# Seven half-size products for eight in the last block of a fused retention and bilinear feed-forward kernel

## The chip, the cores and the metric

The kernel runs on one core of a Trainium2 chip. The metric is the device time of one execution in microseconds. A core has five engines with queues of their own that run side by side and wait for each other through semaphores: TensorE (PE in the profile, its weight loads PEld), VectorE (DVE), ScalarE (ACT), GpSimd (POOL) and SyncE (SP), which here only starts transfers. TensorE writes into PSUM, a small memory of eight banks; GpSimd works only on SBUF, the large one.

## The reference

Retention without softmax over 8 batches, 8 heads, 576 positions and 64 values per head, then a bilinear feed-forward layer over all 4608 tokens:

```
scores = scale * q @ k.T                        # per batch and head
ret    = (scores * decay[h] ** (i - j), i >= j) @ v
x      = ret as (4608, 512)                     # heads side by side
a      = x @ w_a                                # (512, 1536)
b      = x @ w_b                                # (512, 1536)
out    = (a * b) @ w_out                        # (1536, 512)
```

Inputs and output are f32; the kernel multiplies in bf16 and sums in f32.

## The kernel before

Tokens are taken in blocks (512, 256, 256, then seven of 512). `ffn_block` does the feed-forward layer of one block. Between its steps it hands out the retention work of later blocks, which a list `todo` places by a count of matmuls: one unit is a matmul of 512 columns, and an entry is called at the first edge (end of an F step, or of a block) at or after its place. All engines' queues follow the order in which the program emits instructions.

For a block of 512 tokens, with xT the tokens' x, transposed (128 rows x 4 parts x 512):

- First product. For each of 12 columns F of w_a and w_b (128 wide): 4 matmuls into pa (L1141), a copy to bf16 by ScalarE (ha, L1152), 4 matmuls into pb (L1159), and VectorE multiplies the two into hT[:, F] (L1164). That is 96 matmuls of 512 columns a block.
- Row sums. From the seventh block of 256 tokens on, the second product takes seven products for eight (Strassen's scheme in Winograd's form, on quarters of h and w_out). It needs sums of h rows: `row_sums` (L944, recorded on L952) makes five VectorE instructions: three into hsum, two that change hT in place. In the block, they are made for pairs of F 0 to 3 after F = 7 and for pairs 4 and 5 after the last F. `work` hands them out from the list `jobs` within a budget.
- Second product. `rows_mixed` (L982) runs 84 matmuls of 256 columns (`product`, L1022) for two groups g of 256 tokens. The order is: products 3 and 4 on plain h rows, product 1 on the first row sum, then `cross(g)`: products 5 and 2 on the changed h rows; ScalarE keeps what they gave ("crossed", L1034), GpSimd adds the kept "straight" part into the output tile osb (L1045), VectorE subtracts (`lessen`, L1055) and adds the rest (`add_last`, L1062), and SP stores the tile (L972). "straight", "crossed" and "less" are tiles with two buffers each.

In the stretch that matters here, the block before last, retention ends: `outputs_alone` writes the last x rows through VectorE (L808) after F = 9 of that block, in steps taken from the list `later` at F = 10. GpSimd's own retention work, the casts of `ahead` (L562 to L589), is over well before; after it GpSimd has two osb adds per block left. The last block has no retention work beside it.

The stage buffers (tags qf, kf, vf, three each) held the loaded q, k and v of earlier token groups; the last of these loads stands ahead of the last two blocks.

Of the kernel before, what the change touches and what calls it, by code (L numbers as in the profile page):

```python
# [18 lines left out]
def kernel(  # L19
# [10 lines left out]
    nc = tc.nc  # L30
# [4 lines left out]
    NTOK = B * S  # L35
    NC = DM // 128
# [8 lines left out]
    NP = NTOK // 256  # L45
# [34 lines left out]
    stage = pool("stage", 3)  # L80
    nat = pool("nat", 3)
# [5 lines left out]
    ha_pool = pool("ha", 6)  # L87
    o_pool = pool("osb", 4)
    late, early = {}, ExitStack()
# [13 lines left out]
    ps_ffn = pool("ps_ffn", 4, PS)  # L103
    opening, ps_sc, ps_o = ExitStack(), {}, {}
# [17 lines left out]
    wa_sb = big.tile([128, NC, DFF], BF16)  # L122
    wb_sb = big.tile([128, NC, DFF], BF16)
# [18 lines left out]
    shared = {}  # L142
# [117 lines left out]
    def pair_tables(step):  # L260
# [6 lines left out]
        else:  # L267
            for h in (2 * step - 2, 2 * step - 1):
# [33 lines left out]
    def pop():  # L302
        if later:
            later.pop(0)()

    jobs, copies_due = [], []

    def work(budget, up_to=2):
        jobs.sort(key=lambda job: job[0])
        while jobs and jobs[0][0] <= up_to and jobs[0][1] <= budget:  # L310
            _, cost, job = jobs.pop(0)
            job()
            budget -= cost
# [615 lines left out]
    WIDE = DM // 2  # L929
# [11 lines left out]
        out = wo_sums[:, step // 3, p0:p0 + 2]  # L941
        nc.vector.tensor_tensor(out, one, other, op=op)

    def row_sums(hT, sums, p0, p1):  # L944

        even, odd = (hT[:, 2 * p0:2 * p1].rearrange(
            "p (f e) (g k s) -> p e k f g s", e=2, g=2, k=2)[:, e]
            for e in (0, 1))
        a11, a21, a12, a22 = even[:, 0], even[:, 1], odd[:, 0], odd[:, 1]
        to = [sums[:, i, p0:p1] for i in range(3)]  # L950
        return [(1, (p1 - p0) / 8 + 0.2,
                 lambda e=e: nc.vector.tensor_tensor(*e[:3], op=e[3]))  # L952
                for e in ((to[0], a11, a22, ALU.add),
                          (to[2], a12, a22, ALU.subtract),
                          (to[1], a21, a11, ALU.subtract),
                          (a12, a11, a12, ALU.add),
                          (a21, a21, a22, ALU.add))]

    def store_mixed(G, osb, cols=slice(0, 2 * DM), on=nc.sync):

        n = place(G)
        for kp, r0, m, b, s0 in rows_of(n):
            if n in LEFT:
                p0 = kp * 64 + r0 // 2
                m //= 2
            elif kp == 1:
                continue
            else:
                p0, m = 0, 128
            rows = out[b * S + s0:b * S + s0 + 2 * m].rearrange(  # L970
                "(p two) c -> p (two c)", two=2)
            on.dma_start(rows[:, cols],  # L972
                              osb[p0:p0 + m].rearrange("p k c -> p (k c)")
                              [:, cols])
# [3 lines left out]
    def store_formed():  # L978
        while formed:
            store_mixed(*formed.pop(0))  # L980

    def rows_mixed(tok0, hT, sums):  # L982
# [129 lines left out]
            formed.append((pair[g], osbs[g]))  # L1112
        yield 0, True

    def ffn_block(tb, tok0, n, runs):

        xT = x_of(tok0, n)
        hT = h_pool.tile([128, NF, 512], BF16, tag="h", name="hT")
        if tok0 >= 256 * MIXED:
            pools_mixed()  # L1120
            sums = late["hsum"].tile([128, 3, NF // 2, 2, 128], BF16, tag="hsum",
                                  name="hsum")
        f0 = 0
        for count in runs:
            has = {}
            if tb == 0 and f0 == 0:
                for c in range(2, NC):
                    for F in range(count):
                        begin_with(F, c, 1)
            for F in range(f0, f0 + count):  # L1130
                fs = slice(F * 128, (F + 1) * 128)
                pa = (begun[F] if tb == 0 and F in begun else
                      ps_ffn.tile([128, 512], FP32, tag="ab", name="pa"))
                for c in range(NC):
                    if tb == 0 and (F, 0, 0) in begun:
                        if (F, c, 1) not in begun:
                            begin_with(F, c, 1)
                        if c < NC - 1:
                            yield n / 512, False
                        continue  # L1140
                    nc.tensor.matmul(pa[:, 0:n], wa_sb[:, c, fs],  # L1141
                                     xT[:, c],
                                     start=(c == 0), stop=(c == NC - 1))
                    if c < NC - 1:
                        yield n / 512, False
                if n == 512 and tb:
                    pop()
                pass_on(1)
                if F == 2:
                    store_formed()  # L1150
                ha = ha_pool.tile([128, 512], BF16, tag="ha", name="ha")
                nc.scalar.copy(ha[:, 0:n], pa[:, 0:n])  # L1152
                has[F] = ha
                yield n / 512, False
            for F in range(f0, f0 + count):
                fs = slice(F * 128, (F + 1) * 128)
                pb = ps_ffn.tile([128, 512], FP32, tag="ab", name="pb")
                for c in range(NC):
                    nc.tensor.matmul(pb[:, 0:n], wb_sb[:, c, fs],  # L1159
                                     xT[:, c],  # L1160
                                     start=(c == 0), stop=(c == NC - 1))
                    if c < NC - 1:
                        yield n / 512, False
                nc.vector.tensor_tensor(hT[:, F, 0:n], has[F][:, 0:n],  # L1164
                                        pb[:, 0:n], op=ALU.mult)
                pop()
                if tok0 >= 256 * MIXED:
                    if F == 7:
                        jobs.extend(row_sums(hT, sums, 0, 4))
                    elif F == NF - 1:  # L1170
                        jobs.extend(row_sums(hT, sums, 4, 6))
                        work(math.inf, 1)
                work(1.0)
                yield n / 512, True
            f0 += count
        if tb == 0:
            yield from rows_together(tok0, hT, (0, 1))
# [122 lines left out]
    starts, at = {}, 0.0  # L1300
# [42 lines left out]
    def third_turn():  # L1343
        for i in (4, 5):
            transpose_step(i, (Q, "act"), (K, "dve"))

    todo = [(100, early_casts, ()),
            (112.1, cast_step, (5, Q, "act")),
            (124, third_turn, ()), (128, third_states, ()),
            (136, third_outputs, ())]  # L1350
# [34 lines left out]
        casts[n], turns[n] = placed[n] - 96, placed[n] - 58  # L1385
    for fn, places in ((ahead, casts), (turn, turns)):
        todo += [(at, fn, (n,)) for n, at in places.items()]
    todo.sort(key=lambda e: e[0])

    at = 0.0  # L1390
    tok = 0
    for tb, n in enumerate(blocks):
        runs = WCOLS if tb == 0 else [1] * NF
        for cost, edge in ffn_block(tb, tok, n, runs):
            at += cost
            while todo and edge and at >= todo[0][0]:
                _, fn, args = todo.pop(0)
# [33 lines left out]
```

## Time and profile before

Times are microseconds.

| what | value |
|---|---|
| median of 3 runs | 322.25 (321.19 to 322.4) |
| the profiled execution, whole | 320.63 |
| its span, first to last instruction | 318.4 |
| granted TensorE clock in it | 1.000 |
| PE, DVE, ACT, POOL busy | 308.0, 198.9, 145.7, 155.6 |

The page gives busy time by engine, then the same in 40 slices of the span as digits (9 is 90% or more), then the chain of work that ended last, then groups of instructions by line. A group's row reads: line, engine, operation, output <- inputs, output shape and type <- input shape and type, count, busy time, mean length of one. In the trace's timeline the first number is the start in the span, the second the length of the row's instructions together. A start-to-start distance can be a little shorter than a length, as instructions of one engine overlap at their ends.

### The profile page before, as it was taken

To read this page: it belongs to the slowest core of one execution; us is meant where nothing else is said; L and a number is where in the kernel's file an instruction comes from. 1 tells how busy PE (TensorE), PEld (TensorE's weight loads), DVE (VectorE), ACT (ScalarE), POOL (GpSimd) and SP (SyncE) were. 2 spreads that over 40 slices of the span, in tenths; PEclk is the share of its full clock that TensorE was granted. 3 is DMA by queue.
4 is the path that set the end of the run, shared out by engine and by line. 5 is a ranking of instruction groups with operands and counts; after the bars stand their busy time and mean duration, and the time that the engine had idled before them with its cause. 6 is when DMAs were issued, how large, how long until landed. Compare 5 with 4: busy or idle time off the path is not lost.

```text
span 318.4 us, 9134 instructions
## 1 busy us (share of the span) xinstructions
PE 308.0 (97%) x3763; PEld 183.4 (58%) x3799; DVE 198.9 (62%) x376; ACT 145.7 (46%) x324; POOL 155.6 (49%) x169
## 2 busy tenths in 40 slices
PE   7899999999999999999999999999999999999995
PEld 3554457768544554448654864477446744674474
DVE  5745346867757563479658854776567656834563
ACT  7745346536435463454454534544434443423330
POOL 3990078664986577564796089506960300030003
PEclk9999999999999999999999999999999999999999
DMA  8999999999999999999999998974430110012004
GB/s 215 255 203 207 255 231 184 193 207 182 207 178 214 229 218 179 240 193 223 241 280 201 179 229 181 198 164 129 108 68 2 76 61 0 2 74 60 0 1 132
DMA packets 144793, 50.92 MB, mean 160 GB/s; under 512 B 126576, under 2 KB 141680, under 8 KB 144752
## 3 DMA queue, kind: packets, MB, share of 16 engines
q1 hardware_dynamic: 138272, 45.10, 70.9%
q0 software_dynamic: 5808, 4.72, 9.4%
q8 instruction: 29, 0.48, 0.6%
q10 hardware_dynamic: 672, 0.52, 0.5%
q14 instruction: 12, 0.10, 0.1%
HBM read 37.75 MB, written 9.44 MB: 148 GB/s over the span
## 4 chain that ended last, share of the span: by engine, by line
PE 90%; DVE 3%; DMA 2%; issue 2%; POOL 1%; SPq 1%; ACT 0%; DVEq 0%; POOLq 0%
PE pb L1159 29%; PE pa L1141 28%; PE m L1022 16%; PE po L1185 8%; DMA vf<-in_v_dram 2%; PE po L913 2%; PE sc L703 1%; PE o L731 1%; PE o L744 1%; SPq L175 1%; PE kv L632 1%; DVE hT L952 1%; POOL vb L365 1%; DVE sums L659 1%; PE pa L902 1%
## 5 line engine op out<-in xcount | busy, mean ns | idle before, releaser
L1164 DVE TENSOR_TENSOR hT<-ha,pb 128x512 bf16<-128x512 bf16 (+1 forms) x120 | 75.8, 632 | 80.4 <-PE pb L1159 68.5
L1159 PE MATMUL pb<-xT,wb_sb 128*128 128x512 bf16 (+1 forms) x478 | 111.5, 358 | 0.4
L1152 ACT CAST ha<-pa 128x512 bf16<-128x512 f32 (+1 forms) x120 | 64.9, 542 | 96.8 <-PE pa L1141 92.0
L1141 PE MATMUL pa<-xT,wa_sb 128*128 128x512 bf16 (+1 forms) x448 | 106.4, 356 | 1.9 <-issue 1.2
L1159 PEld LDWEIGHTS <-wb_sb 128*128 128x128 bf16 x480 | 46.8, 98 | 47.5 <-issue 1.9
L1141 PEld LDWEIGHTS <-wa_sb 128*128 128x128 bf16 x472 | 45.0, 98 | 43.0 <-DVE sums L659 0.2
L1045 POOL TENSOR_TENSOR osb<-crossed,straight 128x512 f32<-128x512 f32 x12 | 15.2, 1271 | 102.8 <-ACT crossed L1034 96.3
L589 POOL TENSOR_TENSOR vb<-vf,vs 128x1024 bf16<-128x1024 f32 (+1 forms) x17 | 29.6, 1743 | 4.5 <-PE pb L1159 1.7
L1022 PEld LDWEIGHTS <-hT 128*128 128x128 bf16 x288 | 28.1, 98 | 4.7 <-issue 0.3
L562 POOL TENSOR_TENSOR qkb<-qf,qs 64x1024 bf16<-64x1024 f32 x12 | 22.9, 1911 | 14.2 <-DMA qf<-in_q_dram 9.1
L1185 PE MATMUL po<-wo_sb,hT 128*128 128x512 bf16 x113 | 26.7, 379 | 0.8 <-issue 0.6
L1022 PE MATMUL m<-wo_sums,hsum 128*128 128x256 bf16 x216 | 25.7, 273 | 0.0
L567 POOL TENSOR_TENSOR qkb<-qf,qs 64x512 bf16<-64x512 f32 x24 | 24.8, 1052 | 0.7
L1022 PEld LDWEIGHTS <-hsum 128*128 128x128 bf16 x216 | 21.1, 98 | 2.4
L952 DVE TENSOR_TENSOR hsum<-hT 128x1024 bf16<-128x1024 bf16 (+1 forms) x36 | 20.3, 591 | 0.2
L578 POOL CAST qkb<-kf 64x1024 bf16<-64x1024 f32 (+1 forms) x17 | 15.9, 935 | 8.0 <-DMA kf<-in_k_dram 7.1
L712 DVE TENSOR_TENSOR sT<-sc,mask 128x512 bf16<-128x512 f32 x30 | 19.8, 680 | 0.0
L659 DVE TENSOR_TENSOR sums<-kv,sums 128x256 f32<-128x256 f32 x44 | 18.6, 422 | 1.4
L582 POOL CAST qkb<-kf 64x512 bf16<-64x512 f32 (+1 forms) x34 | 18.8, 581 | 0.9
L1185 PEld LDWEIGHTS <-hT 128*128 128x128 bf16 x120 | 11.2, 98 | 12.6
L1022 PE MATMUL m<-wo_sb,hT 128*128 128x256 bf16 x144 | 17.0, 273 | 0.1
L1022 PE MATMUL m<-wo_sums,hT 128*128 128x256 bf16 x144 | 16.9, 273 | 0.0
(111 smaller groups left out, 283.0 us busy)
## 6 DMA issues: line engine op xcount, KB each, us to landing
qf<-in_q_dram SPq DMA_DIRECT2D x32, 256.0 KB, 5.1
vf<-in_v_dram SPq DMA_DIRECT2D x32, 256.0 KB, 5.2
kf<-in_k_dram SPq DMA_DIRECT2D x31, 256.0 KB, 4.9
out_dram<-osb SPq DMA_DIRECT2D x9, 512.0 KB, 4.1
out_dram<-osb SPq DMA_DIRECT2D x22, 128.0 KB, 2.8
wo_sb<-in_moe_w_out_dram POOLq DMA_DIRECT2D x3, 512.0 KB, 16.0
out_dram<-osb SPq DMA_DIRECT2D x6, 256.0 KB, 4.2
qf<-in_q_dram SPq DMA_DIRECT2D x8, 128.0 KB, 4.2
```

Of the source, the lines that this page charges most:

```text
L562: nc.gpsimd.tensor_tensor(per_head(qkb[0:64, Q]), per_head(t[0:64]), by[0:64].unsqueeze(2).to_broadcast([64, 2 * H, D]), op=ALU.mult)
L567: nc.gpsimd.tensor_tensor(per_head(qkb[64:128, Q])[:, 1 - r::2], per_head(t[64:128])[:, r::2], by[64:128, r::2].unsqueeze(2).to_broadcast( ...
L589: nc.gpsimd.tensor_tensor(vb[:, e].rearrange("p (h d) -> p h d", d=D), t[:, e].rearrange("p (h d) -> p h d", d=D), decay[:, at], op=ALU.mult)
L659: nc.vector.tensor_tensor(sums[:, i], own, prev, op=ALU.add)
L712: nc.vector.tensor_tensor(sT[:, on].rearrange("p c k s -> p (c k) s"), sc[on].rearrange("p c k s -> p (c k) s"), mask3.unsqueeze(1).to_bro ...
L952: lambda e=e: nc.vector.tensor_tensor(*e[:3], op=e[3]))
L1022: nc.tensor.matmul(to, rows, cols, start=(begins and p == 0), stop=True, skip_group_check=True)
L1141: nc.tensor.matmul(pa[:, 0:n], wa_sb[:, c, fs], xT[:, c], start=(c == 0), stop=(c == NC - 1))
L1152: nc.scalar.copy(ha[:, 0:n], pa[:, 0:n])
L1159: nc.tensor.matmul(pb[:, 0:n], wb_sb[:, c, fs], xT[:, c], start=(c == 0), stop=(c == NC - 1))
L1164: nc.vector.tensor_tensor(hT[:, F, 0:n], has[F][:, 0:n], pb[:, 0:n], op=ALU.mult)
L1185: nc.tensor.matmul(po, hT[:, F, u * 128:(u + 1) * 128], wo_sb[:, F], start=(F == 0), stop=(F == NF - 1))
```

## The change

The first product of the last block (tokens 4096 to 4607) is taken in pairs of h rows, F = 2p and 2p + 1. For pairs 0, 1, 3 and 4 the same scheme of seven products for eight is used on quarters of x (two halves of its 512 inner rows, two groups of 256 tokens) and of the weights (two halves of the inner rows, two columns F). Each of the seven products is 4 matmuls of 256 columns: for w_a and w_b (m), and for two parts c. Pairs 2 and 5 stay as they were.

- `combine`: GpSimd makes four sums of weight quarters per pair and matrix, 32 instructions on 128x256 bf16. They lie in tiles that take buffers of the tags qf and kf, and are placed from 20 units ahead of the block before last, 2.8 units apart.
- `combine_rows`: GpSimd makes four sums of x quarters, 128x512 bf16, in a buffer of the tag qkb, placed 44 units ahead of the last block. With the edges as they are, they are emitted after F = 11 of the block before last, ahead of its second product and behind the last writes of x.
- In the last block a pair uses three PSUM places (main, side, aside). ScalarE copies products 1, 5 and 6 out as f32 into buffers of "straight", "less" and "crossed"; VectorE adds the second half of each sum from PSUM; GpSimd multiplies the a half with the b half into hT. The fourth quarter is copied by ScalarE and multiplied by VectorE as before. `ORDER` writes the order of the products of two pairs and of the plain steps "a" and "b" out by hand.
- Row sums of the last block are made per pair (256 elements) instead of per four and two pairs, and handed out by `SHARE`. `SHARED` is 0, so all of them stay on VectorE.

The core of the diff:

```diff
-    def row_sums(hT, sums, p0, p1):
+    def row_sums(hT, sums, p0, p1, shared=0):
...
+        ways = ((to[2], a12, a22, ALU.subtract),
+                (to[1], a21, a11, ALU.subtract),
+                (to[0], a11, a22, ALU.add),
+                (a12, a11, a12, ALU.add),
+                (a21, a21, a22, ALU.add))
+        order = (2, 0, 1, 3, 4)
...
+        return [(0.9 if i == 2 and p1 == p0 + 1 else 1, (p1 - p0) / 8 + 0.2,
+                 lambda e=ways[i]: nc.vector.tensor_tensor(*e[:3], op=e[3]))
+                for i in order if i >= shared]
...
+    def combine(p, m, i):
+        if p not in combos:
+            combos[p] = stage.tile([128, 2, 4, 2, 128], BF16,
+                                   tag=("qf", "kf")[len(combos) % 2], name="combo")
+        (a11, a12), (a21, a22) = quarter_weights(m, p)
+        s3, s1, s2, s4 = (combos[p][:, m, k] for k in range(4))
+        out, one, other, op = [(s3, a11, a21, ALU.subtract),
+                               (s1, a21, a22, ALU.add),
+                               (s2, a22, s3, ALU.subtract),
+                               (s4, a12, s2, ALU.subtract)][i]
+        nc.gpsimd.tensor_tensor(out, one, other, op=op)
...
+        x = x_of(256 * (NP - 2), 512)
+        (b11, b12), (b21, b22) = [[x[:, c:c + 2, 256 * g:256 * g + 256]
+                                   for g in (0, 1)] for c in (0, 2)]
+        t1, t3, t2, t4 = (row_combos[0][:, k] for k in range(4))
+        out, one, other, op = [(t1, b12, b11, ALU.subtract),
+                               (t3, b22, b12, ALU.subtract),
+                               (t2, b11, t3, ALU.add),
+                               (t4, b21, t2, ALU.subtract)][i]
+        nc.gpsimd.tensor_tensor(out, one, other, op=op)
...
+            to = st["aside" if way == 2 else
+                    "side" if way in (3, 5) else "main"]
+            for m in (0, 1):
+                w, x = {1: (a11, xT[:, 0:2, g0]), 2: (a12, xT[:, 2:4, g0]),
+                        3: (s4, xT[:, 2:4, g1]), 4: (a22, t4), 5: (s1, t1),
+                        6: (s2, t2), 7: (s3, t3)}[way]
+                for c in (0, 1):
+                    nc.tensor.matmul(to[:, m], w[:, c], x[:, c],
+                                     start=(way in (1, 2, 5) and m == c == 0),
+                                     stop=True, skip_group_check=True)
...
+        def gated(t, own, to):
+            nc.vector.tensor_tensor(t, own, t, op=ALU.add)
+            nc.gpsimd.tensor_tensor(to, t[:, 0], t[:, 1], op=ALU.mult)
...
+            if way == 1:
+                st["first"] = keep("straight", st["main"])
+            elif way == 5:
+                st["third"] = keep("less", st["side"])
+            elif way == 6:
+                st["second"] = keep("crossed", st["main"])
+            elif way == 2:
+                gated(st["first"], st["aside"], hT[:, F0, g0])
+            elif way == 3:
+                gated(st["second"], st["side"], hT[:, F0, g1])
+            elif way == 7:
+                gated(st["third"], st["main"], hT[:, F1, g1])
+            else:
+                nc.scalar.copy(ha[:, g0], st["main"][:, 0])
+                nc.vector.tensor_tensor(hT[:, F1, g0], ha[:, g0],
+                                        st["main"][:, 1], op=ALU.mult)
...
+    ORDER = ((1, 0), (5, 0), (2, 0), (6, 0), (1, 1), (3, 0), (7, 0), (5, 1),
+             (2, 1), (6, 1), (4, 0), ("a", 4), (3, 1), (7, 1), ("b", 4),
+             ("a", 5), (4, 1), ("b", 5),
+             (1, 3), (5, 3), (2, 3), (6, 3), (1, 4), (3, 3), (7, 3), (5, 4),
+             (2, 4), (6, 4), (4, 3), ("a", 10), (3, 4), (7, 4), ("b", 10),
+             ("a", 11), (4, 4), ("b", 11))
+    SHARE = {1: 0, 5: 0, 2: 0, 6: 0.4, 3: 0, 7: 0.4, 4: 0, "a": 0.4, "b": 0.7}
...
+        if tok0 == NTOK - 512:
+            yield from last_layer(xT, hT, sums)
+            yield from rows_mixed(tok0, hT, sums)
+            return
...
+    todo += [(starts[NP - 4] - 20 + 2.8 * i, combine,
+              (SEVENS[i // 8], i // 4 % 2, i % 4))
+             for i in range(8 * len(SEVENS))]
+    todo += [(starts[NP - 2] - 44 + 0.1 * i, combine_rows, (i,))
+             for i in range(4)]
```

More of the change, by code (lines that the diff above doesn't have):

```diff
@@ L950, in row_sums @@
         to = [sums[:, i, p0:p1] for i in range(3)]
[L951 to L957, printed above, removed]
+        ways = ((to[2], a12, a22, ALU.subtract),
[4 more added lines that the diff above has]
+        order = (2, 0, 1, 3, 4)
+        for i in range(shared):
+            out, one, other, op = ways[i]
+            nc.gpsimd.tensor_tensor(out, one, other, op=op)
+        return [(0.9 if i == 2 and p1 == p0 + 1 else 1, (p1 - p0) / 8 + 0.2,
+                 lambda e=ways[i]: nc.vector.tensor_tensor(*e[:3], op=e[3]))
+                for i in order if i >= shared]
     def store_mixed(G, osb, cols=slice(0, 2 * DM), on=nc.sync):
@@ L1113, in rows_mixed, with quarter_weights @@
         yield 0, True
+    SEVENS = (0, 1, 3, 4)
+    SHARED = 0
+    combos = {}
+    def quarter_weights(m, p):
+        w = (wa_sb, wb_sb)[m]
+        return [[w[:, c:c + 2, 128 * F:128 * F + 128] for c in (0, 2)]
+                for F in (2 * p, 2 * p + 1)]
+    def combine(p, m, i):
[9 more added lines that the diff above has]
+        nc.gpsimd.tensor_tensor(out, one, other, op=op)
@@ new lines, with combine_rows @@
+    row_combos = []
+    def combine_rows(i):
+        if not row_combos:
+            row_combos.append(nat.tile([128, 4, 2, 256], BF16, tag="qkb",
+                                       name="rows"))
+        x = x_of(256 * (NP - 2), 512)
[6 more added lines that the diff above has]
+                               (t4, b21, t2, ALU.subtract)][i]
+        nc.gpsimd.tensor_tensor(out, one, other, op=op)
@@ new lines, in layer_mixed, with quarter, keep, after @@
+    def layer_mixed(xT, hT):
+        t1, t3, t2, t4 = (row_combos[0][:, k] for k in range(4))
+        g0, g1 = slice(0, 256), slice(256, 512)
+        state = {}
+        def quarter(p, way):
+            if way == 1:
+                state[p] = {
+                    "main": ps_ffn.tile([128, 2, 256], FP32, tag="ab",
+                                        name="lm"),
+                    "side": ps_sc[0].tile([128, 2, 256], FP32, tag="sc",
+                                          name="ls")}
+            st = state[p]
+            if way == 2:
+                st["aside"] = ps_o[0].tile([128, 2, 2, 256], FP32, tag="o",
+                                           name="la")[:, 0]
+            to = st["aside" if way == 2 else
+                    "side" if way in (3, 5) else "main"]
+            for m in (0, 1):
+                (a11, a12), (_, a22) = quarter_weights(m, p)
+                s3, s1, s2, s4 = (combos[p][:, m, k] for k in range(4))
+                w, x = {1: (a11, xT[:, 0:2, g0]), 2: (a12, xT[:, 2:4, g0]),
[5 more added lines that the diff above has]
+                                     stop=True, skip_group_check=True)
+                    yield 0.5, False
+        def keep(name, own):
+            t = late[name].tile([128, 2, WIDE], FP32, tag=name, name=name)
+            nc.scalar.copy(t, own)
+            return t
+        def gated(t, own, to):
+            nc.vector.tensor_tensor(t, own, t, op=ALU.add)
+            nc.gpsimd.tensor_tensor(to, t[:, 0], t[:, 1], op=ALU.mult)
+        def after(p, way):
+            st = state[p]
+            F0, F1 = 2 * p, 2 * p + 1
+            if way == 1:
+                st["first"] = keep("straight", st["main"])
[10 more added lines that the diff above has]
+            else:
+                ha = ha_pool.tile([128, 512], BF16, tag="ha", name="ha")
+                nc.scalar.copy(ha[:, g0], st["main"][:, 0])
+                nc.vector.tensor_tensor(hT[:, F1, g0], ha[:, g0],
+                                        st["main"][:, 1], op=ALU.mult)
+        return quarter, after
@@ new lines, with last_layer @@
+    ORDER = ((1, 0), (5, 0), (2, 0), (6, 0), (1, 1), (3, 0), (7, 0), (5, 1),
[5 more added lines that the diff above has]
+    SHARE = {1: 0, 5: 0, 2: 0, 6: 0.4, 3: 0, 7: 0.4, 4: 0, "a": 0.4, "b": 0.7}
+    def last_layer(xT, hT, sums):
+        quarter, after = layer_mixed(xT, hT)
+        has = {}
+        for i, (way, at) in enumerate(ORDER):
+            done = None
+            if way in ("a", "b"):
+                F = at
+                p1 = ps_ffn.tile([128, 512], FP32, tag="ab", name="p" + way)
+                for c in range(NC):
+                    w = wa_sb if way == "a" else wb_sb
+                    nc.tensor.matmul(p1, w[:, c, F * 128:F * 128 + 128],
+                                     xT[:, c], start=(c == 0),
+                                     stop=(c == NC - 1))
+                    yield 1, False
+                if way == "a":
+                    has[F] = ha_pool.tile([128, 512], BF16, tag="ha",
+                                          name="ha")
+                    nc.scalar.copy(has[F], p1)
+                else:
+                    nc.vector.tensor_tensor(hT[:, F], has[F], p1, op=ALU.mult)
+                    if F % 2:
+                        done = F // 2
+            else:
+                yield from quarter(at, way)
+                after(at, way)
+                if way == 4:
+                    done = at
+            if i == 3:
+                store_formed()
+            if done is not None:
+                jobs.extend(row_sums(hT, sums, done, done + 1, SHARED))
+            work(SHARE[way])
+        work(math.inf, 1)
```

## The prediction

> **What bounds the kernel now.** I read the page's shares first, then the chain that ended last, then the three stretches that the change touches, and last the rows of GpSimd and VectorE in them.
>
> ```profile
> PE 308.0 (97%) x3763; PEld 183.4 (58%) x3799; DVE 198.9 (62%) x376; ACT 145.7 (46%) x324; POOL 155.6 (49%) x169
> POOL 3990078664986577564796089506960300030003
> ```
>
> TensorE is the bound: 97% busy. POOL's digits, tenths of 40 slices, show it nearly idle in the last quarter.
>
> ```profile
> 275.42 9.17 PE m L1022 x84
> 305.31 9.18 PE m L1022 x84
> ```
>
> The chain of waits is TensorE's work to nine tenths. Columns: start, length. A second product takes 84 matmuls of 256 columns in 9.17 us, 0.1093 us each.
>
> ```profile
> 252.20:284.40 32.20, 31.99 (x342) 19.39 (x344) 19.82 (x39) 11.66 (x24) 2.54 (x2) 1.00 0.08 34
> 284.40:305.10 20.70, 20.59 (x96) 9.39 (x97) 10.81 (x17) 7.02 (x12) 0.00 (x0) 1.00 0.16 52
> ```
>
> Stretches: the block before last, and the first product of the last block. Columns: length, then busy us (instructions) of PE, PEld, DVE, ACT, POOL, clock, DMA share, GB/s. The 20.70 us are 96 matmuls of 512 columns, 0.2155 us each, with nothing between them; POOL does nothing. These matmuls are what the change thins out; the stretch above is where its preparation goes.
>
> ```profile
> 271.90 0.68 DVE L952 TENSOR_TENSOR hsum<-hT 128x1024 bf16<-128x1024 bf16 x1
> 272.50 1.28 DVE L952 TENSOR_TENSOR hT<-hT 128x1024 bf16<-128x1024 bf16 x2
> 273.71 0.74 DVE L808 TENSOR_TENSOR xT<-o,both 128x256 bf16<-128x256 f32 x2
> 274.38 0.67 DVE L1164 TENSOR_TENSOR hT<-ha,pb 128x512 bf16<-128x512 bf16 x1
> 274.97 0.74 DVE L808 TENSOR_TENSOR xT<-o,both 128x256 bf16<-128x256 f32 x2
> 275.63 0.68 DVE L1164 TENSOR_TENSOR hT<-ha,pb 128x512 bf16<-128x512 bf16 x1
> 276.35 1.10 DVE L952 TENSOR_TENSOR hsum<-hT 128x512 bf16<-128x512 bf16 x3
> 277.36 0.76 DVE L952 TENSOR_TENSOR hT<-hT 128x512 bf16<-128x512 bf16 x2
> ```
>
> Start, length. VectorE works without a pause from 271.90 to 278.1 at the end of the block before last. Start to start, a row sum of 1024 elements costs 0.60 us, one of 512 0.337 us. TensorE begins the second product at 275.25.
>
> ```profile
> 144.45 3.01 DVE L952 TENSOR_TENSOR hT<-hT 128x1024 bf16<-128x1024 bf16 x2
> ...
> 143.08 1.52 POOL L582 CAST qkb<-kf 64x512 bf16<-64x512 f32 x2
> 144.69 2.22 POOL L589 TENSOR_TENSOR vb<-vf,vs 128x1024 bf16<-128x1024 f32 x1
> ...
> 170.87 1.95 DVE L952 TENSOR_TENSOR hsum<-hT 128x1024 bf16<-128x1024 bf16 x1
> ...
> 170.37 1.90 POOL L589 TENSOR_TENSOR vb<-vf,vs 128x1024 bf16<-128x1024 f32 x1
> ```
>
> These decide the case. The row sum at 170.87 took 1.95 us where others take 0.68: POOL's multiply ended at 172.27 and the sum 0.55 us later. At 144.45 two sums took 3.01 us instead of 1.28: the first ran 0.6 us, POOL's multiply, issued at 144.69 and stretched from 1.90 to 2.22, came in between and ended at 146.91, then the second ran. So a VectorE instruction with both inputs in SBUF and a GpSimd instruction exclude each other, and with both queued they alternate.
>
> **The change part by part.**
>
> Matmuls removed. A pair with seven products issues 7 x 2 x 2 = 28 matmuls of 256 columns, 28 x 0.1093 = 3.06 us, instead of 16 x 0.2155 = 3.45. Four pairs: -1.55 us. All of it lies on the path. Each small matmul has its own weight load (98 ns), hidden in the second product at the same pitch.
>
> Evictions of the four pairs. Three ScalarE copies (0.49 us start to start: "straight" 1.07 us x2 shows 0.49) and a small one (0.27), three VectorE adds with one input in PSUM (0.61) and a small multiply (0.34), three POOL multiplies. VectorE in the last block: 4 x (1.83 + 0.34) + 4 x 0.61 = 11.1 us, plus 30 row sums of 256 elements. Those are on no row; the step from 1024 to 512 gives 0.337 - 0.263/2 = 0.205 us, and the other end is no shrinking, 0.337. I take 0.205, as the two rows lie on a line: 6.2 us, of which 15 sums (3.1) fall behind the last matmul. So 14.2 us of VectorE beside 19.1 of TensorE. ScalarE: 12 x 0.49 + 4 x 0.27 + 4 x 0.49 = 8.9. All of this is covered while VectorE keeps its 5 us of slack. POOL's 12 multiplies have ends 0.615 (multiply with a broadcast factor, bf16 result, 128x256) and 0.722 (add of f32 tiles, 128x256): 7.4 to 8.7 us, and each may hold up a row sum: 15 sums in the layer x chance 0.45 x half a multiply = 2.3 us, inside the slack.
>
> New waits on TensorE. Product 6 of a pair waits for the copy of product 1: three products of 0.437 us later, while the copy ends 0.437 + 0.2 + 0.58 us after its start, 0.09 us in time (0.2 is what lies between a matmul's slot and its copy, 287.01 to 287.21). Product 7 and 4 wait for ScalarE and VectorE with over 0.5 us to spare. Cost 0, and if ScalarE is late by x, x per pair.
>
> The tail. The order leaves 15 sums of the last pairs behind the final multiply. The last modified rows are needed by the first crossing product: 30 matmuls (3.28 us) and five more (0.55) after the layer, 3.83; sum 14 of 15 ends at 0.2 + 0.61 + 14 x 0.205 + 0.08 = 3.76. Cost 0; with 0.337 it is 1.8 us late.
>
> Weight sums on POOL. 32 instructions 128x256, bf16 adds: ends 0.615 and 0.722 again (a cast of one tile, 0.40, is a floor); I take 0.66, between a bf16 result and an add. They stand behind the block's two osb adds that end at 252.2 and run through: 32 x 0.64 (start to start is 0.04 less than the length: three L365 in 1.76) = 20.5, plus 1.8 for three row sums of VectorE that take turns: done about 274.5. On the path nothing. But VectorE's sums at 271.90 and the two at 272.50 take turns with them: about 0.33 + 0.66 us, so that what follows is 1.0 us late: x complete at 276.7 instead of 275.7, the last multiply at 277.3, where the products of the last pair want it at 275.25 + 20 x 0.1093 = 277.4. Just covered.
>
> Row combinations on POOL. Four instructions 128x512; ends 1.04 (vb, 128x512) and 1.27 (osb, f32), I take 1.15. They wait for the last x write, 276.7, and behind them stand both osb adds (281.36 before), the stores of that block on SP, and, through the reuse of "straight", ScalarE's first copy in the last block. VectorE comes to its five small sums at 277.3. Now they alternate: combination 276.75 to 277.9, sum to 278.25, combination to 279.4, sum to 279.75, combination to 280.9, sum to 281.25, combination to 282.4, and only then the first modified h rows, 282.75. Before they were there at 277.7. TensorE wants them 40 matmuls after 275.25, at 279.62: a stall of 282.75 + 0.15 - 279.62 = 3.3 us. With 1.04 and 0.615: 2.6; with 1.27 and 0.722: 4.0. What is late next, the crossed copies, osb adds and stores, moves along; POOL's first osb add ends about 285.4, ahead of the last block's first copy.
>
> The Trainium skill, "SBUF — State Buffer", section "Who interferes with whom", has this as an exclusive lock: a VectorE instruction with two SBUF inputs and a GpSimd instruction that reads SBUF block each other whole, and issue order decides who waits. The rows above agree (1.95 for 0.68 us); without that lock the sum would be -1.55 alone, with it +1.75.
>
> Sum: -1.55 + 3.3 = +1.75, against the profiled execution's 320.63 (span 318.4, 2.2 around it): 322.4. That execution lies 1.6 under the median of the runs, 322.25; the same step from the median gives 324.0.
>
> **The rivals.**
>
> A, forecast: the row combinations take turns with the block's row sums. From +1.0 (low prices) to +2.5 (high).
>
> B, faster: VectorE keeps its turn while it has sums queued. The combinations then fall behind the five sums (278.1 + 4 x 1.15 = 282.7, early enough for the last block), the modified rows are there before 279.6 and no stall is left: -1.55, or 320.7. It decides at any price of a combination. Against it stands the one clear case at 144.45; for it, that there is only one. While they alternate, a cheap combination does not reach as far: at the floor of a cast (0.61 for 128x512) the rows come at 276.7 + 4 x 0.61 + 4 x 0.34 = 280.5, a stall of 1.0 and a sum of -0.5; only under 0.4 is nothing left of it.
>
> C, POOL late as a whole: if a weight sum costs 0.75 or more, 32 of them end past 277, the combinations past 283, and the osb adds hold ScalarE's first copies and with them product 6. Each 0.01 us is 0.32 us: at 0.8, +3 to +4, or 325.5. Against it: no row of this size is over 0.722.
>
> D, the tail: the 256-element sums don't shrink; 1.8 us more on top of A or B: 325.8, or 322.5 without A. For it: no such form is in the trace.
>
> **How the numbers follow.** A 0.55, B 0.22, C 0.11, D 0.12. A's own range is 323.2 to 324.9. No difference of under 0.5% (1.6 us) can be told from no change. A is above it in about 0.37 of its 0.55 and within in 0.18; B ends at its edge, -0.48%: 0.10 faster, 0.12 same; C slower; D 0.07 slower, 0.05 same. Faster 0.10, same 0.35, slower 0.55. The range that leaves out about 2 in 10 goes from B (320.5) to C and D (326.0).
>
> **What would show it.** In the last block the first product's matmuls span 19.1 us instead of 20.7, with no gap at product 6: the first term. In the block before, the four 128x512 combinations lie between small row sums, each sum lasting over 1 us, and TensorE has one gap of 2.6 to 4.0 us at the crossing product: the second. If the sums stay at 0.4 us and there is no gap, B is right and I am wrong by 3 us. A first gap at product 6 of the last block is C; a gap at the last crossing product is D.

## The result and the profile after

The changed kernel takes 322.76 us in the median of 17 executions (321.07 to 324.21), the kernel before on the same chip 320.92 us (17 executions, 319.98 to 322.4). The medians lie 1.84 us apart, 0.57%; the ratio estimated from all executions is 1.0049, 95% interval 1.0029 to 1.0068. So it is slower, at the very edge of the 0.5% that the prediction called no change. One slow execution of the kernel before, of 1129.69 us, is left out of the medians below. The profiled execution took 324.21 us, its span 322.5 us, at a mean granted clock of 0.994.

The page of the changed kernel, busy shares and POOL's digits:

```profile
PE 311.7 (97%) x3847; PEld 189.0 (59%) x3847; DVE 209.8 (65%) x404; ACT 148.9 (46%) x332; POOL 191.7 (59%) x217
POOL 4791068653995668564696079506960699765313
```

POOL is now at work in the last quarter, where it was idle. TensorE has 84 more matmuls, all of half size.

The chain that ended last (start, length):

```profile
280.21 3.47 DVE hsum L961 x3
283.68 1.30 DVE hT L961
285.02 4.98 PE m L1027 x44
...
309.18 9.19 PE m L1027 x84
```

Before, the chain ran through TensorE alone here. Now it leaves TensorE for four of VectorE's small row sums, 4.8 us.

The same two stretches, with the columns as before:

```profile
255.53:289.84 34.31, 31.95 (x343) 18.91 (x340) 24.35 (x38) 11.66 (x24) 29.43 (x38) 1.00 0.08 32
289.84:309.01 19.17, 19.17 (x146) 14.07 (x144) 15.50 (x36) 10.18 (x20) 8.66 (x12) 1.00 0.18 56
```

The first product of the last block takes 19.17 us instead of 20.70, with TensorE busy throughout: the saving is there, 1.53 us. The block before last has grown, and TensorE is idle in it for 2.4 us.

Where it is idle shows in the timeline (start, length, engine, line; rows of several short windows, put in order of their start):

```profile
279.66 1.15 POOL L1157 TENSOR_TENSOR rows<-xT 128x512 bf16<-128x512 bf16 x1 [1.48 <-DVE xT L808]
280.21 0.89 DVE L961 TENSOR_TENSOR hsum<-hT 128x512 bf16<-128x512 bf16 x1
280.77 1.34 POOL L1157 TENSOR_TENSOR rows<-xT 128x512 bf16<-128x512 bf16 x1
281.02 1.37 DVE L961 TENSOR_TENSOR hsum<-hT 128x512 bf16<-128x512 bf16 x1
282.07 0.60 PE L1027 MATMUL m<-wo_sb,hT 128*128 128x256 bf16 x4
282.19 1.21 POOL L1157 TENSOR_TENSOR rows<-xT,rows 128x512 bf16<-128x512 bf16 x1
282.31 1.36 DVE L961 TENSOR_TENSOR hsum<-hT 128x512 bf16<-128x512 bf16 x1
283.48 1.21 POOL L1157 TENSOR_TENSOR rows<-xT,rows 128x512 bf16<-128x512 bf16 x1
283.60 1.37 DVE L961 TENSOR_TENSOR hT<-hT 128x512 bf16<-128x512 bf16 x1
285.02 2.36 PE L1027 MATMUL m<-wo_sb,hT 128*128 128x256 bf16 x20 [2.36 <-DVE hT L961]
```

One combination, one sum, and so on. A sum of 0.34 us shows as 1.37 us: it ends 0.29 us after the combination beside it, so the time for which it is held up is counted as its own length. TensorE comes to the crossing product at 282.07, runs four matmuls (to 282.51, at 0.1093 us each) and stands until 285.02: 2.51 us. (The row's 2.36 counts from the modelled end of the fourth matmul.)

This execution's span is 4.1 us longer than that of the one shown of before. 2.88 us of it lie ahead of the block before last, in code that the change doesn't touch: at 14 to 16 us TensorE waited some 1 us more for ScalarE, and from 18 to 22 us its granted clock was near half. So executions are compared below by the **late stretch**, from the start of the crossing product (the 24 matmuls "m<-wo_sb,hT") to the end of VectorE's last instruction. Before, that is 279.18 to 314.94, 35.76 us; in the changed kernel 282.07 to 318.81, 36.74 us, 0.98 longer. That is the stall less the saving, 2.51 - 1.53. The 0.2 us that are left lie in the last stores.

### The profile page after: what moved, and what is told of

It reads as the page before. It is cut to its first block, busy times and chain, and to the rows that moved or that the text cites. A ratio compares the mean times of both kernels' runs of the same rounds, so it can differ in the third digit from the quotient of the medians.

```text
span 322.5 us, 9351 instructions
## 1 busy us (share of the span) xinstructions
PE 311.7 (97%) x3847; PEld 189.0 (59%) x3847; DVE 209.8 (65%) x404; ACT 148.9 (46%) x332; POOL 191.7 (59%) x217
## 4 chain that ended last, share of the span: by engine, by line
PE 89%; DVE 3%; SPq 2%; DMA 2%; issue 1%; ACT 1%; DVEq 0%
PE pb L1313 25%; PE pa L1295 25%; PE m L1027 16%; PE po L1339 8%; SPq L175 2%; PE lm L1185 2%; DMA vf<-in_v_dram 2%; PE po L913 2%; PE sc L703 2%; PE o L744 1%; PE o L731 1%; DVE hsum L961 1%; PE kv L632 1%; PE ls L1185 1%; PE pa L1241 1%
## 5 line engine op out<-in xcount | busy, mean ns | idle before, releaser
L1318 DVE TENSOR_TENSOR hT<-ha,pb 128x512 bf16<-128x512 bf16 (+1 forms) x108 | 67.4, 626 | 71.3 <-PE pb L1313 60.0
L1313 PE MATMUL pb<-xT,wb_sb 128*128 128x512 bf16 (+1 forms) x432 | 99.8, 357 | 0.1
L1295 PE MATMUL pa<-xT,wa_sb 128*128 128x512 bf16 (+1 forms) x424 | 97.6, 355 | 0.0
L1306 ACT CAST ha<-pa 128x512 bf16<-128x512 f32 (+1 forms) x108 | 57.9, 537 | 83.6 <-PE pa L1295 79.9
L1313 PEld LDWEIGHTS <-wb_sb 128*128 128x128 bf16 x432 | 42.3, 98 | 42.3 <-issue 2.5
L1295 PEld LDWEIGHTS <-wa_sb 128*128 128x128 bf16 x424 | 40.3, 98 | 37.6 <-DVE sums L659 0.2
L1339 PE MATMUL po<-wo_sb,hT 128*128 128x512 bf16 x120 | 27.8, 380 | 0.0
L961 DVE TENSOR_TENSOR hsum<-hT 128x256 bf16<-128x256 bf16 (+2 forms) x48 | 25.5, 559 | 0.4
L582 POOL CAST qkb<-kf 64x512 bf16<-64x512 f32 (+1 forms) x34 | 19.1, 590 | 0.9
```

The source lines that it names most:

```text
L582: nc.gpsimd.tensor_copy(to[:, :, 1 - r], fro[:, :, r])
L961: lambda e=ways[i]: nc.vector.tensor_tensor(*e[:3], op=e[3]))
L1295: nc.tensor.matmul(pa[:, 0:n], wa_sb[:, c, fs], xT[:, c], start=(c == 0), stop=(c == NC - 1))
L1313: nc.tensor.matmul(pb[:, 0:n], wb_sb[:, c, fs], xT[:, c], start=(c == 0), stop=(c == NC - 1))
L1318: nc.vector.tensor_tensor(hT[:, F, 0:n], has[F][:, 0:n], pb[:, 0:n], op=ALU.mult)
L1339: nc.tensor.matmul(po, hT[:, F, u * 128:(u + 1) * 128], wo_sb[:, F], start=(F == 0), stop=(F == NF - 1))
```

## The experiments

The theory was that GpSimd's four combinations take turns with the five small row sums, and that nothing else of the change costs anything. Each kernel was measured beside the kernel before on its chip. "Gap" is TensorE's stand at the crossing product, counted as above. The late stretch is that of the one execution in the kept trace. e10 and e11, single executions, stand in the text.

| kernel | median us, beside before's | ratio, 95% interval | gap us | late stretch us |
|---|---|---|---|---|
| before | | 1 | 0 | 35.76 |
| changed | 322.76, 320.92 | 1.0049 (1.0029 to 1.0068) | 2.51 | 36.74 |
| e1, combinations on VectorE | 319.11, 321.08 | 0.9944 (0.9923 to 0.9964) | 0 | 34.22 |
| e2, combinations behind the sums | 319.66, 321.08 | 0.9957 (0.9940 to 0.9973) | 0 | 34.61 |
| e3, combinations in halves | 319.80, 321.08 | 0.9962 (0.9949 to 0.9976) | 0.62 | 35.00 |
| e4, preparation alone | 324.68, 321.08 | 1.0119 (1.0077 to 1.0161) | 2.51 | 39.77 |
| e5, weight sums alone | 321.42, 321.42 | 0.9995 (0.9971 to 1.0019) | 0 | 35.76 |
| e6, e1 with late sums | 322.94, 321.42 | 1.0051 (1.0025 to 1.0076) | 2.39 | 36.62 |
| e7, e1 with later sums | 327.39, 321.42 | 1.0175 (1.0139 to 1.0211) | 6.12 | 42.65 |
| e8, seven products for six pairs | 328.51, 321.42 | 1.0238 (1.0197 to 1.0280) | 1.26 | 41.55 |
| e9, seven products for five pairs | 321.28, 321.06 | 1.0013 (0.9997 to 1.0029) | 0 | 36.26 |

**e1: the combinations on VectorE.**

```diff
     def combine_rows(i):
...
-        nc.gpsimd.tensor_tensor(out, one, other, op=op)
+        nc.vector.tensor_tensor(out, one, other, op=op)
```

> The four combinations of the last block's inputs (128x512) are formed by VectorE, behind its five small row sums of the block before last, and not by GpSimd beside them; nothing else differs from the changed kernel. Theory (the small sums and GpSimd's combinations take turns, and the 2.51 us that TensorE loses at the crossing product of the block before last is that): the small sums run at the 0.4 us apiece that they had before, TensorE has no gap there (under 0.3 us), and the time is the changed kernel's less 2.5 us, 1.0 to 1.6 us under the kernel before's, from 1.55 us less matrix work. Rival one (the first products of the last block are not really shorter on the path, and the loss is spread): the time moves by less than 1 us against the changed kernel. Rival two (the sums are late because the block's inputs are late, not because of the combinations): a gap of 1 us or more stays at the crossing product.

The timeline of e1:

```profile
278.29 1.10 DVE L961 TENSOR_TENSOR hsum<-hT 128x512 bf16<-128x512 bf16 x3
279.30 0.76 DVE L961 TENSOR_TENSOR hT<-hT 128x512 bf16<-128x512 bf16 x2
279.97 0.76 DVE L1157 TENSOR_TENSOR rows<-xT 128x512 bf16<-128x512 bf16 x2
280.76 0.89 DVE L1157 TENSOR_TENSOR rows<-xT,rows 128x512 bf16<-128x512 bf16 x2
...
280.14 2.78 PE L1027 MATMUL m<-wo_sb,hT 128*128 128x256 bf16 x24
```

Sums at 0.34 us apiece, as before the change, and 24 matmuls in one piece. The four combinations take VectorE 1.7 us; on GpSimd they took 5. The late stretch is 1.54 us shorter than before's (expected 1.55). Both rivals fall, and this kernel beats both others: 1.97 us under the kernel before, with an interval of 1.2 to 2.5 that holds the 1.54. It is more than the expected 1.0 to 1.6. The medians of e2 and e3, 1.42 and 1.28 us under, also lie 0.3 to 0.5 us lower than their late stretches say, inside their intervals or at the edge, and 0.2 to 0.3 lower than expected. What that is stays open; e5, with the weight sums alone, shows no such gain, though its interval would hide one.

**e2: the combinations on GpSimd, behind the sums.**

```diff
+            nc.gpsimd.tensor_copy(row_combos[0][:, 0, 0, 0:128],
+                                  last_h[0][:, NF - 2, 384:512])
```

The copy stands ahead of the first combination and reads the last changed h rows; what it writes is overwritten by that combination.

> The four combinations stay on GpSimd, but a small copy of 128x128 that reads the last of the small row sums' results stands ahead of them, so that they begin only after all five sums. Theory of the turns: the sums run at about 0.4 us apiece, no gap at the crossing product (under 0.4 us); the combinations end near 5 us after the last sum, which makes GpSimd's two additions into the stores' buffer late by 2 to 3 us, so that ScalarE's first copies of the last block wait and product 6 of the first pair stands still for 0.3 to 1.0 us; the time is 0.5 to 1.2 us under the kernel before's. Rival (GpSimd's work as a whole is late, whoever goes first): the loss at product 6 is 2 us or more and the time is like the changed kernel's, 0.5 to 1.5 us over the kernel before's.

```profile
280.11 0.29 POOL L1149 COPY rows<-hT 128x128 bf16<-128x128 bf16 x1 [3.85 <-DVE hT L961]
280.48 2.27 POOL L1159 TENSOR_TENSOR rows<-xT 128x512 bf16<-128x512 bf16 x2
282.82 2.38 POOL L1159 TENSOR_TENSOR rows<-xT,rows 128x512 bf16<-128x512 bf16 x2
285.16 2.50 POOL L1050 TENSOR_TENSOR osb<-crossed,straight 128x512 f32<-128x512 f32 x2
...
287.10 0.60 PE L1187 MATMUL lm<-rows,combo 128*128 128x256 bf16 x4 [0.25 <-ACT straight L1194]
```

In e2's timeline the combinations come after the sums, the two osb adds behind them (285.16, in e1 282.32), and product 6 stands for 0.25 us on the copy of product 1, which had waited for the first osb add. The late stretch is 0.40 us longer than e1's. So the same four instructions on the same engine cost 2.51 us among the sums and 0.4 behind them; the chain by which rival C would have cost exists, with that small price.

**e3: each combination in two halves.**

```diff
-        nc.gpsimd.tensor_tensor(out, one, other, op=op)
+        for s0 in (0, 128):
+            nc.gpsimd.tensor_tensor(*(t[:, :, s0:s0 + 128]
+                                      for t in (out, one, other)), op=op)
```

> Each of the four combinations is issued as two instructions of 128x256, eight in place of four, the same elements in all. If the engines take strict turns, each small row sum waits for one GpSimd instruction of half the length (0.65 to 0.75 us for 1.15 to 1.34): four turns of about 0.75 in place of 1.29 us, TensorE's gap at the crossing product 0.4 to 1.0 us in place of 2.5, and the time 1.5 to 2.1 us under the changed kernel's, 0.2 to 1.0 us under the kernel before's. Rival (what matters is the amount of GpSimd's work that lies ahead of the sums or beside them, whatever its pieces): the gap stays at 2.0 us or more and the time within 0.5 us of the changed kernel's.

```profile
276.85 3.12 POOL L1158 TENSOR_TENSOR rows<-xT 128x256 bf16<-128x256 bf16 x4 [1.47 <-DVE xT L808]
277.40 2.04 DVE L961 TENSOR_TENSOR hsum<-hT 128x512 bf16<-128x512 bf16 x3
279.37 1.69 DVE L961 TENSOR_TENSOR hT<-hT 128x512 bf16<-128x512 bf16 x2
279.93 2.91 POOL L1158 TENSOR_TENSOR rows<-xT,rows 128x256 bf16<-128x256 bf16 x4
280.31 2.51 PE L1027 MATMUL m<-wo_sb,hT 128*128 128x256 bf16 x20 [0.46 <-DVE hT L961]
```

GpSimd does the same work, no sooner and no less of it (6.0 us for 5.0). But the sums now end 0.81 us apart where they ended 1.29 apart: the first four are done 2.9 us after the first begins (277.40 to 280.25), where they took 4.8, and the gap falls from 2.51 to 0.62 us. What a sum waits for is one GpSimd instruction, not GpSimd's work: the rival falls. Cutting the pieces in two got 1.75 us of the late stretch back (36.74 to 35.00).

**e4: the preparation alone.** The branch to the new last layer is taken out.

```diff
-        if tok0 == NTOK - 512:
-            yield from last_layer(xT, hT, sums)
-            yield from rows_mixed(tok0, hT, sums)
-            return
```

> The last block is computed as in the kernel before, with eight products for every pair; GpSimd still forms the weights' sums and the four combinations, whose results nothing uses. Theory: the stall at the crossing product stays at 2.5 us, and the 1.55 us of matrix work is not saved, so the time is 2.2 to 2.8 us over the kernel before's and about 1.5 us over the changed kernel's. Rival (the seven products save less than 1 us, or nothing): the time is within 0.5 us of the changed kernel's.

It came out 3.60 us over the kernel before, about 1 us more than expected, with an interval of 2.5 to 5.2 us. The gap is the expected 2.51 us. The rest is in e4's stretches behind it (window, length, then busy us (instructions) of PE, PEld, DVE, ACT and POOL, then the granted clock):

```profile
284.00:286.00 2.00, 1.58 (x8) 1.14 (x9) 0.70 (x2) 0.00 (x0) 0.09 (x1) 0.52 0.00 0
286.00:288.00 2.00, 2.00 (x14) 1.50 (x13) 0.69 (x1) 0.59 (x1) 0.99 (x1) 0.62 0.00 0
```

Of the clock 0.48 and 0.38 are missing in stretches of 2 us, which makes 3.4 us at half speed, from 284.1 to 287.5. TensorE is back at work from 284.42, so it works 3.1 us at half speed and loses 1.5. With it the late stretch is 4.02 us longer than before's, near 2.51 + 1.5. No step of the prediction has that. e6, e7, e10 and e11 were made for it.

**e5: the weight sums alone.** As e4, without the combinations.

```diff
-    todo += [(starts[NP - 2] - 44 + 0.1 * i, combine_rows, (i,))
-             for i in range(4)]
```

> The last block is computed as in the kernel before, with eight products for every pair; of the change only GpSimd's 32 sums of weights are kept, whose results nothing uses. The prediction's step 5 says that they cost nothing: the time is within 0.3 us of the kernel before's, the late x rows are still complete before they are needed, and there is no gap at the crossing product. Rival (they slow VectorE's sums and the late x rows far enough): 1.0 us or more over the kernel before's, with a gap on TensorE in the block before last. If e1's gain beyond 1.55 us came from this part, the time would be 0.4 us or more under the kernel before's.

No difference can be seen: 0.9995, with an interval from 0.9 us less to 0.6 us more. The trace says it more sharply: no gap at the crossing product, and a late stretch of 35.76 us, that of the kernel before. The 32 GpSimd instructions cost nothing there.

**e6 and e7: a stall without GpSimd.** To e1, n more copies of the third small row sum, which write the same result again (n is 7 in e6, 15 in e7):

```diff
-                        jobs.extend(row_sums(hT, sums, 4, 6))
+                        five = row_sums(hT, sums, 4, 6)
+                        if tok0 == NTOK - 1024:
+                            five[2:2] = 7 * [five[2]]
+                        jobs.extend(five)
```

> The kernel e1 (combinations on VectorE, no gap), with VectorE making the third of the five small row sums of the block before last eight times instead of once: seven more instructions of 0.34 us from start to start, so that the changed h rows are 2.4 us late at the crossing product, with no GpSimd work beside them. It tells the stall itself from what else the changed kernel does. Theory one (a stall of this length costs its length and, in more than a third of the executions, a spell of low TensorE clock worth some 1.7 us): 2.4 us plus 0.5 to 1.5 us over e1 in the median, with granted clocks of 0.992 to 0.995 in several executions. Theory two (the low clock of the changed kernel has another cause, in its GpSimd work or by chance): 2.2 to 2.6 us over e1, and granted clocks of 0.997 or more throughout, as in e1.

```profile
278.25 4.31 DVE L961 TENSOR_TENSOR hsum<-hT 128x512 bf16<-128x512 bf16 x10
282.48 0.75 DVE L961 TENSOR_TENSOR hT<-hT 128x512 bf16<-128x512 bf16 x2
282.95 2.36 PE L1027 MATMUL m<-wo_sb,hT 128*128 128x256 bf16 x20 [2.24 <-DVE hT L961]
```

With a gap of 2.39 us and no GpSimd beside it, e6 has the changed kernel's time: 1.0051 against 1.0049. In 7 of 12 executions its mean clock was 0.988 to 0.994, in five 0.999 or 1.0; the medians of the two groups are 323.48 and 321.82 us. The changed kernel splits in the same way: 11 of 17 at 0.992 to 0.994, median 323.26, and six at 0.997 to 0.999, median 321.63. e6 is 3.5 us over e1 by the differences to the kernel before (expected 2.9 to 3.9). Theory one holds: the low clock needs no GpSimd work. The traced execution of e6 is one without a spell, so where the spells of the others lie is not seen.

> As e6, with fifteen more instructions instead of seven: the changed h rows are 5.1 us late. If a TensorE gap brings a spell of low clock, and more surely the longer it is: low clock behind the gap in all or nearly all executions (granted clock 0.995 or less), and the time is 6.3 to 7.3 us over e1's. If the low clock has nothing to do with the gap: 4.9 to 5.4 us over e1's, clocks 0.997 or more.

The gap came out longer than meant, 6.12 us, since the repeated sums start 0.46 us apart, not 0.34; so the time is 7.9 us over e1's, above the range expected. All five executions have clocks of 0.988 to 0.992. e7's stretches:

```profile
285.00:286.00 1.00, 0.00 (x0) 0.00 (x0) 0.93 (x3) 0.00 (x0) 0.00 (x0) 0.70 0.00 0
286.00:287.00 1.00, 0.00 (x0) 0.00 (x0) 0.93 (x4) 0.00 (x0) 0.00 (x0) 0.50 0.00 0
...
288.00:290.00 2.00, 2.00 (x11) 1.34 (x10) 1.27 (x4) 0.59 (x1) 0.00 (x0) 0.50 0.00 0
290.00:292.00 2.00, 2.00 (x11) 1.40 (x10) 0.69 (x1) 0.05 (x1) 1.26 (x1) 0.50 0.00 0
292.00:293.00 1.00, 1.00 (x10) 0.85 (x9) 0.43 (x1) 0.54 (x1) 0.39 (x1) 0.88 0.00 0
```

TensorE stopped at 281.35; some 4 us later the clock is halved, and stays so for 6.8 us, 4.8 of them after the work went on at 287.47. The late stretch is 8.44 us longer than e1's, the gap and 2.3 us of lost clock.

**e10 and e11: the changed kernel twice more,** unaltered, for the place of the spell.

> The changed kernel as it is, for the place of the low TensorE clock. If the gap at the crossing product brings it, an execution with a granted clock of 0.992 to 0.995 shows a spell near half speed within 10 us behind the gap, and one with 0.997 or more shows none anywhere. If it belongs to the first 30 us, as in the profiled execution shown above, the spell lies there and not behind the gap.

> The same as e10, a second execution: with a granted clock of 0.992 to 0.995 a spell near half speed behind the gap, if the gap brings it; near the start, if the start brings it; none at 0.997 or more.

e10 took 321.39 us at a clock of 0.999, with a gap of 2.52 us and no spell; e11 took 324.10 us at 0.994. e11's stretches behind its gap, which lasted from 280.74 to 283.25:

```profile
284.00:285.00 1.00, 1.00 (x9) 0.80 (x8) 0.05 (x1) 0.59 (x1) 0.01 (x1) 0.72 0.00 0
285.00:286.00 1.00, 1.00 (x7) 0.67 (x6) 0.64 (x1) 0.00 (x0) 1.00 (x1) 0.50 0.00 0
286.00:287.00 1.00, 1.00 (x6) 0.70 (x5) 0.00 (x0) 0.37 (x1) 0.25 (x1) 0.50 0.00 0
287.00:288.00 1.00, 1.00 (x8) 0.70 (x6) 0.69 (x1) 0.21 (x1) 0.71 (x1) 0.58 0.00 0
```

Here the spell does lie behind the gap, begins 1.2 us after the work went on and lasts 3.4 us (0.56 + 2 + 0.84), which loses 1.7 us: the late stretch is 38.40 us, in e10 36.74. So the same gap brings it in some executions and not in others; the last section has what sets them apart. The execution shown first had its spell at 18 to 22 us, and none behind its gap; e4's had one in each place. The early place is not the gap's doing: e9's profiled execution, without the gap, has an early one too. What brings that on is open; executions of the kernel before were at 0.995 or less in 4 of 60, so it is rare there.

**e8 and e9: seven products for more pairs,** on top of e1. e8 takes all six, in the order of two pairs without plain steps between; e9 takes five, with product 4 of a pair moved behind three products of the next.

```diff
-    SEVENS = (0, 1, 3, 4)
+    SEVENS = (0, 1, 2, 3, 4)
...
+    ORDER = (((1, 0), (5, 0), (2, 0), (6, 0))
+             + tuple((way, p - q) for p in (1, 2, 3, 4) for way, q in
+                     ((1, 0), (3, 1), (7, 1), (5, 0), (2, 0), (6, 0), (4, 1)))
+             + (("a", 10), (3, 4), (7, 4), ("b", 10), ("a", 11), (4, 4),
+                ("b", 11)))
```

> The kernel e1 with seven products for all six pairs of the last block instead of four; 16 more sums of weights on GpSimd, begun 8.6 us earlier. TensorE's work falls by another 0.78 us (28 x 0.1093 for 16 x 0.2155 us, two pairs). VectorE's work for two pairs is six additions of 0.69, two multiplications of 0.42 and ten row sums of 0.205 us from start to start, some 7.0 us by lengths and 6.6 us by starts, against 6.12 us of matmuls. If VectorE's lag of 0.5 us per two pairs only fills its idle time: 0.5 to 0.8 us under e1's time. If VectorE bounds the block: TensorE waits for it in the products of the third two pairs and at the last row sums, and the time is 0.5 to 1.5 us over e1's.

> The kernel e1 with seven products for five pairs, and an order without two products of one pair in a row: product 4 of a pair follows three products of the next one, and the plain steps of the sixth pair stand between the last products. Eight more sums of weights on GpSimd, made in its idle time before the block before last. TensorE saves another 0.39 us (28 x 0.1093 for 16 x 0.2155). VectorE's work in the first product is then about 18.9 us by starts, against 18.8 us of matmuls. If VectorE still fits: 0.2 to 0.4 us under e1's time. If it is the bound: TensorE waits for it at product 4 of the later pairs or at the last row sums, and the time is 0.5 to 2 us over e1's.

TensorE's waits from 280 us on (engine and line, what it waited for: us in all, times, longest), e8 first, then e9:

```profile
PE lm L1185 <- DVE less L1196: 6.2, 3, 2.2
PE m L1027 <- DVE hT L961: 1.1, 1, 1.1
```

```profile
PE lm L1185 <- DVE less L1196: 1.8, 3, 0.8
```

In both, product 4 waits for VectorE to have read product 7 from the same PSUM place. In e8 it stands right behind product 7, so each of three pairs pays some 2 us, far more than the expectation made of it; and its weight sums ran to 283 us, beside the small row sums, for another 1.1. e9 mends the order, and VectorE still comes late: its difference to the kernel before is 2.2 us above e1's, just over the upper end of what was expected. e8's is 9.1 above it; five of its six executions have clocks of 0.988 to 0.993, the traced one 0.999. By these two runs the plain steps between the pairs, which the change keeps, are VectorE's time to catch up; no run changes them alone.

## Why the prediction was right, and where not

- **Matmuls removed, -1.55.** Right: 19.17 us for 20.70, and the late stretch of e1 is 1.54 us shorter.
- **Evictions, waits at product 6, the tail: 0.** Right. VectorE had 15.50 us of work in the 19.17 (predicted 14.2 of 19.1), and TensorE no gap. The GpSimd multiplies took 0.72 to 0.77 us, at the upper end of 0.722 and just over it. The row sums of 256 elements, on no row of before, start 0.202 us apart (taken: 0.205). In the changed kernel's timeline, the last four of them:

```profile
312.04 0.49 DVE L961 TENSOR_TENSOR hsum<-hT 128x256 bf16<-128x256 bf16 x2
312.45 0.49 DVE L961 TENSOR_TENSOR hT<-hT 128x256 bf16<-128x256 bf16 x2
```

- **Weight sums: 0.** Right (e5). They took 0.63 us start to start where independent, 0.74 where one needs the one before, 23.2 us in all for the predicted 22.3. The late x rows were complete at 279.57, or 276.69 without the 2.88 us of the early part: predicted 276.7.
- **Row combinations: a stall of 3.3 us.** The mechanism is right, shown from three sides (e1, e2, e3), and the size is off: 2.51 us, just under the range of 2.6 to 4.0. The term that failed is the turn. It was taken as 1.15 us for a combination and 0.35 for a sum, 1.50 in all; measured, the sums end 1.29 us apart, with combinations of 1.15 to 1.34 us. Alone, in e2, the combinations start 1.11 us apart, or 1.23 where one needs the one before. So of a sum's 0.34 us only 0.06 to 0.18 adds to the turn, and four turns are 0.8 us cheaper. Whether sum and combination overlap by the rest, or the recorded length of a combination holds time in which it leaves SBUF alone, no run here shows. The alternation itself is what the forecast took from one row at 144.45. The Trainium skill, "SBUF — State Buffer", section "Who interferes with whom", has it as an exclusive lock; the trace agrees in so far as no sum ends before the combination that it stands beside.
- **A term was left out:** the low clock, 1.6 us between the two groups' medians, in 11 of 17 executions, about 1.0 us of the mean. How much of it is the gap's in the changed kernel is not shown: of its three executions with a trace (two of them beside the 17), e11 has its spell behind the gap, the one shown first an early one, and e10 none.

So the sum of +1.75 against +1.84 measured is closer than its parts, by luck: 0.8 us too much for the stall and some 1.0 us too little for the clock cancel. The predicted time, 324.0, lies 1.2 us over the measured one because it was counted from the median of three executions, 322.25; over 17 that median is 320.92. So the measured 322.76 lies below the range given for A, 323.2 to 324.9, though A is what happened; only the wide range from B to D holds it.

Of the rivals, B (VectorE keeps its turn) is refuted by the timeline; C by the weight sums' price, on average under 0.75 us, and by the missing gap at product 6, with its chain seen small in e2; and D by the 0.202 us.

## What to carry to other kernels

Before work is moved to an idle GpSimd, look at which VectorE instructions with both inputs in SBUF run beside it, and whether TensorE waits for one of them: there each VectorE instruction can cost the length of a whole GpSimd instruction. The remedy is the order (behind the urgent sums), the size of the pieces, or VectorE itself, which did these four in a third of the time. And a gap on TensorE of two and a half microseconds can cost 1.5 us or more beyond its length, so a median that moves more than the trace's gaps explain is to be read with the granted clock of every execution.

## What was not expected of the hardware

The granted clock fell to half behind short gaps. With a gap of 2.4 to 2.5 us the mean clock was 0.995 or less in 11 of 17 (changed), 4 of 6 (e4) and 7 of 12 executions (e6), with one of 6.1 us in 5 of 5, with one of 0.6 us in none of 12 (e3). Early spells are among these; without any gap there it was 4 of 60 (before), 1 of 12 (e5), 1 of 13 (e9) and none of 15 (e1, e2). The spells that the traces show last 3.4 us, or 6.8 us in e7, twice as long.

The Trainium skill, "TensorE: Matmul & The Clock Gate", section "What's actually happening", describes a free-running window of about 3.4 us over which TensorE's activity is judged. The lengths of 3.4 and 6.8 us agree with it, and so do the times at which the clock changes. In the kept traces of the changed kernel, e4, e7, e9 and e11 the full-speed stretches between two spells, or from the first full clock to the first spell, last 10.24, 13.65, 262.83 and 279.89 us, which is 3, 4, 77 and 82 times 3.413. So each trace has a grid of 3.413 us, and its place can be counted on from any change of the clock.

Where the grid cuts the gap goes with what follows. In e11, 2.23 us of the gap of 2.51 lie in one stretch of the grid, in e4 2.19, in e7 a whole stretch: the clock falls at the end of that stretch. In the changed kernel's execution shown first it is 1.89 us, in e10 1.79, in e6 1.22, and of e8's three waits at product 4 at most 2.07: no spell. So among these dense matmuls some 2.1 to 2.2 of 3.41 us divide the two, in seven traces; no run shifts the gap against the grid on purpose. The early spells don't follow it: TensorE was idle for only 0.9 to 1.4 us of the stretch ahead of them, in a time of many small matmuls.

The Trainium skill's rule of thumb on the same page, no idle gaps over about 3.4 us (section "HAM oscillation — how this bites in real kernels"), is too generous here: a gap of 2.51 us was enough in e4 and e11.
